# Block 0's second feed-forward product in plain float32, with w_out split piece by piece behind it

## The chip, the cores and the metric

The kernel runs on one core of a Trainium2 chip. The metric is the device time of one execution, in microseconds. Five engines work side by side, each through its own row of instructions in a fixed order: TensorE (PE, with the weight loads PEld), VectorE (DVE), ScalarE (ACT), GpSimd (POOL) and SyncE (SP), which here only starts DMAs. PE writes to PSUM, the others work in SBUF and, apart from GpSimd, in PSUM. An instruction that needs another engine's result waits at the head of its row, and everything behind it waits too.

## What is computed

A linear attention with positive random features, and behind it a feed-forward layer with GELU, all in float32:

```python
def phi(x):
    proj = np.einsum('bhsd,md->bhsm', x, omega)
    sq = np.sum(x * x, axis=-1, keepdims=True) / 2.0
    h = proj - sq
    h = h - np.max(h, axis=-1, keepdims=True)
    return np.exp(h) / np.sqrt(m)
...
num = np.einsum('bhsm,bhmd->bhsd', q_p, kv)
den = np.einsum('bhsm,bhm->bhs', q_p, z)[..., None] + 1e-06
x = (num / den).transpose(0, 2, 1, 3).reshape(B * S, H * D)
h = x @ w_in
g = 0.5 * h * (1.0 + erf(h * inv_sqrt2))
return (g @ w_out).astype(np.float32)
```

Batch 8, 8 heads, 576 tokens a batch, head dimension 64, 128 features; 4608 tokens in all, w_in 512 x 2048, w_out 2048 x 512.

## The kernel before

**Two streams.** The attention runs in 32 units: a batch and a pair of heads. The first four units (mode 0, batch 0) and the next four (mode 1, batch 1) compute with plain float32 matmuls; the others (mode 2) with operands split into two narrower halves. The feed-forward part runs in 12 blocks of 384 tokens. For a block, 16 chunks c of 128 hidden features go by: `mm1` gives h (12 matmuls: w_in high and low by x high and low), `act_high` the GELU, and `mm2`, two chunks later, adds the chunk's part to three accumulators of 128 tokens by 512 columns.

**Precision by halves.** Matmul operands of type fp32r are narrower than float32. So a product is made of three: high by high, low by high, high by low. For the second product, `act_high` writes g (line 629) and its fp32r cast gh (630, ScalarE), `act_low` the rest gl (635, VectorE), and `mm2` issues lines 645 to 647: woh by gh, woh by gl, wol by gh.

**The weights.** Both weight matrices come as 64-bit words in 16 pieces each, are turned into float32 on the chip and split into halves, in the steps of `w_events`: `w_load` (line 124, a DMA into one of three buffers raw), `w_scale` (131 and 132, ScalarE), `w_bits` (136 and 137, VectorE), `w_round` (141, GpSimd, which also frees the raw buffer), `w_high` (148 on GpSimd or 152 on ScalarE for w_out by turns, 148 or 150 for w_in) and `w_low` (155, on VectorE for w_out, on GpSimd for w_in). The float32 piece stands in one of two buffers wb, and the halves wih, wil, woh, wol stay for the whole kernel.

**A mode-1 unit.** `proj_mid` projects (533, 544) and takes the maximum (594) and the difference (596) on VectorE into the one tile et; `exps` (320, ScalarE); `kv_plain` (571, PE; its copy 574), `kvz_plain` (581, copies 586 and 587 on VectorE); `q_trans` (439, PE, which reads et) and `q_copy` (446); `num` (459), `den` (475), `div` (485 to 494) to the feed-forward's input xs. For a mode-2 unit GpSimd makes r (242), the parts of v (343 to 361), the shift of k (266) and kh (373).

**What sets the order.** Every step is put on a list with a time by hand (`at`), one unit of time being roughly one product step of PE; the list is sorted, and a scheduler lays it out on the engines' rows, moving steps that are ready into places that it believes idle. Block 0's chunk c is due at 6c and its second product at 6c + 15.3; piece i of w_out has its steps at 5.5i. The mode-1 units are due at 5, 25.5, 46 and 66.5, the first mode-2 unit at 115, with its preparation from 85. So block 0, the mode-1 units and nearly all of the weight pieces share the first sixth of the run.

Of the kernel before, what the change touches and what calls it, by code (L numbers as in the profile page):

```python
# [19 lines left out]
P = 128  # L20
T = 384
# [7 lines left out]
def favor_attention_ffn(ctx: ExitStack, tc: tile.TileContext, qT, kT, v, omT, w_in, w_out, out):  # L29
# [31 lines left out]
    wih = cp.tile([P, NJ, F], F32R, name="wih")  # L61
    wil = cp.tile([P, NJ, F], F32R, name="wil")
    woh = cp.tile([P, NF, DM], F32R, name="woh")
    wol = cp.tile([P, NF, DM], F32R, name="wol")
    xt = cp.tile([P, 2, 2, S], F32, name="xt")
    xf = xt.rearrange("p a h s -> p (a h s)")
    x2 = xt[:, :, 0]
# [32 lines left out]
    def need(*ks):  # L100
        assert all(k in done for k in ks), ks
# [30 lines left out]
        nc.scalar.activation(pc.lo, pc.lo.bitcast(U32), AF.Copy, scale=2.0 ** -29)  # L132

    def w_bits(pc):
        pc.b = dp[0].tile([P, pc.n], I32, tag="wb", name="wb", bufs=2)
        nc.vector.tensor_scalar(pc.b, pc.hi, 3, None, op0=ALU.logical_shift_left)
        nc.vector.scalar_tensor_tensor(pc.b, pc.hi, -2 ** 31, pc.b, op0=ALU.bitwise_and, op1=ALU.bitwise_or)  # L137

    def w_round(pc):

        nc.gpsimd.tensor_tensor(pc.b, pc.b, pc.lo, op=ALU.add)  # L141

    def w_high(pc):
        pc.w = pc.b.bitcast(F32)
        if pc.win:
            pc.w = pc.w.rearrange("p (j w) -> p j w", j=NJ)
        if pc.e[0] is nc.gpsimd:
            nc.gpsimd.tensor_scalar(pc.wh, pc.w, 1.0, 1.0, op0=ALU.mult, op1=ALU.mult)
        elif pc.e[0] is nc.vector:
            nc.vector.tensor_copy(pc.wh, pc.w)  # L150
        else:
            nc.scalar.copy(pc.wh, pc.w)
# [5 lines left out]
    def piece(win, i, n):  # L158
        pc = Obj()
        pc.win, pc.n, pc.i = win, n, i  # L160

        if win:
            pc.e = (nc.gpsimd, nc.gpsimd) if i < WEARLY else (nc.vector, nc.gpsimd)
        else:
            pc.e = (nc.scalar, nc.gpsimd)[i % 2], nc.vector
        if win:
            m = n // NJ
            sl = slice(i * m, (i + 1) * m)
            pc.src, pc.wh, pc.wl = wi_raw[:, :, 2 * i * m:2 * (i + 1) * m], wih[:, :, sl], wil[:, :, sl]
        else:  # L170
            c, r = divmod(i * n, DM)
            pc.src, pc.wh, pc.wl = wo_raw[:, c, 2 * r:2 * (r + n)], woh[:, c, r:r + n], wol[:, c, r:r + n]
        return pc

    def w_events(pc, t, ts):
        for fn, dt in zip((w_load, w_scale, w_bits, w_round, w_high, w_low), ts):
            at(t + dt, fn, pc)
# [445 lines left out]

    def act_high(n, c):
        h = hs.pop((n, c))
        g = mp[0].tile([P, T], F32, tag="g", name="g", bufs=1)
        gh = mp[0].tile([P, T], F32R, tag="gh", name="gh", bufs=3)
        gl = mp[0].tile([P, T], F32R, tag="gl", name="gl", bufs=3)
        nc.scalar.activation(g, h[:, 0:T], AF.Gelu)  # L629
        nc.scalar.copy(gh, g)  # L630
        gs[n, c] = (g, gh, gl)
# [4 lines left out]
        done.add(('g', n, c))  # L636

    def mm2(n, c, i, c0=0, c1=DM):
        need(('w', False, c), ('g', n, c))
        if c == 0:  # L640
            accs[n, i, c0] = ps_at() if c0 else ps_acc()
        acc = accs[n, i, c0][:, 0:c1 - c0]
        _, gh, gl = gs[n, c]
        s = slice(i * P, (i + 1) * P)
        nc.tensor.matmul(acc, gh[:, s], woh[:, c, c0:c1], start=(c == 0), stop=False)  # L645
        nc.tensor.matmul(acc, gl[:, s], woh[:, c, c0:c1], start=False, stop=False)  # L646
        nc.tensor.matmul(acc, gh[:, s], wol[:, c, c0:c1], start=False, stop=(c == NF - 1))  # L647
        done.add(('a', n, c, i, c0))

    def store(n, i, c0=0, c1=DM):  # L650
        need(*[('a', n, c, i, c0) for c in range(NF)])
        if c0 == 0:
            os[0] = mp[0].tile([P, DM], F32, tag="raw", name="o", bufs=3)
        o = os[0][:, c0:c1]
        nc.vector.tensor_copy(o, accs.pop((n, i, c0))[:, 0:c1 - c0])
        nc.sync.dma_start(out[n * T + i * P:n * T + (i + 1) * P, c0:c1], o)
# [29 lines left out]

    for i in range(NF):
        w_events(piece(True, i, 512), BASE + 1 + 5 * i if i < WEARLY else SUB * i - 27, (-6, 0, 1, 2, 3, 4))
        w_events(piece(False, i, 512), 5.5 * i, (-7, 0, 1, 2, 3, 4))


    bursts = [5 + 20.5 * k for k in range(NJ)] + [115 + 35 * k for k in range(len(units) - 2 * NJ)]
# [53 lines left out]
    for n in range(NBLK):  # L746
        for j in range(NJ):
            t = n * NF * SUB - (5, 4, 3, 3)[j]
            at(t, block_high, n, j)
            at(t + 0.6, block_low, n, j)  # L750
        for c in range(NF):
            t = (n * NF + c) * SUB
            for s in range(3):

                at(t + s + 0.3 if (n, c) != (0, 1) or s == 2 else 1.5 + 0.3 * s, mm1, n, c, s)
            at(t + 3.4, act_high, n, c)
            at(t + 4.5, act_low, n, c)
            if (n, c) >= (NBLK - 1, NF - 1 - LAG):
                continue
            for i in range(NTT):  # L760
                for cut in cuts(n, i):
                    at(t + SUB * LAG + 3.3 + i, mm2, n, c, i, *cut)
                    if c == NF - 1:
                        at(t + SUB * LAG + 4 + i, store, n, i, *cut)
# [50 lines left out]
```

## Time and profile before

| | us |
|---|---|
| median of three runs | 1100.27 (1098.75 to 1100.88) |
| the profiled execution's own time | 1100.79 |
| its span, first to last instruction | 1098.9 |
| busy: PE, VectorE, ScalarE, GpSimd | 1049.1, 789.7, 618.0, 482.4 |
| mean granted PE clock | 0.992 |

PE is busy for 95% of the span. Its records overlap, since matmuls are pipelined and their ends are modelled, so its share of busy time says little about short stops; the distance from one start to the next says more. A row of the windows view gives, for a stretch of time, each engine's busy time with its number of instructions, the granted PE clock as a fraction, and the DMA engines' share and rate. A row of the groups view gives line, engine, operation, out<-in, shapes and count, then busy time, mean length in ns, and idle time of the engine just before, with what ended it. A timeline row gives start, length, engine and line, with idle time before it in brackets. "SPq" is SyncE issuing a DMA.

### The profile page before, as it was taken

How to read it: one execution, taken by the hardware profiler on the slowest of the kernel's cores; microseconds unless marked ns; L12 is line 12 of the kernel's file. 1: busy time of each engine (PE TensorE's matmuls, PEld its weight loads, DVE VectorE, ACT ScalarE, POOL GpSimd, SP SyncE). 2: the span in 40 equal slices, each digit the busy share in tenths (PEclk: the TensorE clock that was granted, in tenths of full speed). 3: DMA queues.
4: the chain of work that ended last, by engine and by line, in shares of the span. 5: the costliest groups of instructions: out<-in, count | busy, mean ns of one | idle time of the engine just before them, and what ended most of it. 6: DMA issues, size and time to landing. Idle time of an engine off the chain costs nothing.

```text
span 1098.9 us, 17294 instructions
## 1 busy us (share of the span) xinstructions
PE 1049.1 (95%) x6022; PEld 906.3 (82%) x6022; DVE 789.7 (72%) x1780; ACT 618.0 (56%) x1310; POOL 482.4 (44%) x554
## 2 busy tenths in 40 slices
PE   8897899999999999999899999999999999999998
PEld 6675678888888888888778788878888888998998
DVE  5879887778878887877888878888887877411211
ACT  7856665666556466666546666654666655322321
POOL 4624546544455565444456544445654444000000
PEclk9989999999999999999999999999999999999999
DMA  8534532211211211211212211122121110000000
GB/s 232 169 110 150 164 117 60 70 44 44 75 44 56 84 56 52 62 50 47 72 56 56 75 32 56 57 62 55 56 74 41 49 63 1 1 29 1 30 1 30
DMA packets 46279, 70.92 MB, mean 65 GB/s; under 512 B 13680, under 2 KB 22256, under 8 KB 46192
## 3 DMA queue, kind: packets, MB, share of 16 engines
q1 hardware_dynamic: 46192, 69.81, 21.2%
q8 instruction: 48, 0.79, 0.3%
q14 instruction: 39, 0.32, 0.1%
HBM read 60.36 MB, written 9.44 MB: 64 GB/s over the span
## 4 chain that ended last, share of the span: by engine, by line
PE 64%; DVE 18%; ACT 2%; issue 2%; POOL 1%; POOLq 0%; ACTq 0%; DVEq 0%
PE h L622 27%; PE acc L647 9%; PE acc L646 9%; PE acc L645 9%; PE at L468 3%; PE at L400 3%; DVE gl L635 2%; DVE et L285 2%; PE at L249 2%; DVE mx L287 2%; PE at L277 1%; DVE xs L497 1%; DVE rt L485 1%; DVE rc L486 1%; DVE rt L488 1%
## 5 line engine op out<-in xcount | busy, mean ns | idle before, releaser
L622 PE MATMUL h<-xh,wih 128*128 128x384 f32 x768 | 263.2, 343 | 0.0
L622 PE MATMUL h<-xl,wih 128*128 128x384 f32 x768 | 262.5, 342 | 0.0
L622 PE MATMUL h<-xh,wil 128*128 128x384 f32 x768 | 262.0, 341 | 0.0
L645 PE MATMUL acc<-woh,gh 128*128 128x512 f32 (+1 forms) x576 | 230.8, 401 | 0.0
L647 PE MATMUL acc<-wol,gh 128*128 128x512 f32 (+1 forms) x576 | 226.6, 393 | 0.0
L646 PE MATMUL acc<-woh,gl 128*128 128x512 f32 (+1 forms) x576 | 226.2, 393 | 0.0
L635 DVE TENSOR_TENSOR gl<-g,gh 128x384 fp32r<-128x384 f32 x192 | 128.6, 670 | 121.1 <-ACT gh L630 120.6
L242 POOL TENSOR_TENSOR r<-xt,r 64x256 fp32r<-64x256 f32 (+2 forms) x216 | 173.8, 813 | 59.5 <-ACT r L236 46.4
L629 ACT ACTIVATE g<-h 128x384 f32<-128x384 f32 x192 | 94.4, 491 | 170.0 <-PE h L622 161.0
L373 POOL TENSOR_SCALAR kh<-et 128x256 f16<-128x256 f32 (+1 forms) x120 | 50.2, 425 | 280.8 <-ACT et L320 176.0
L622 PEld LDWEIGHTS h<-xh,wih 128*128 128x128 f32 x768 | 145.1, 189 | 7.7 <-issue 1.8
L622 PEld LDWEIGHTS h<-xh,wil 128*128 128x128 f32 x768 | 145.0, 189 | 6.3 <-issue 0.9
L622 PEld LDWEIGHTS h<-xl,wih 128*128 128x128 f32 x768 | 145.3, 189 | 1.3 <-issue 0.9
L647 PEld LDWEIGHTS acc<-wol,gh 128*128 128x128 f32 x576 | 108.3, 188 | 23.9
L645 PEld LDWEIGHTS acc<-woh,gh 128*128 128x128 f32 x576 | 108.5, 188 | 14.6 <-issue 1.5
L646 PEld LDWEIGHTS acc<-woh,gl 128*128 128x128 f32 x576 | 108.6, 189 | 12.8 <-issue 0.4
L236 ACT CAST r<-xt 128x256 fp32r<-128x256 f32 (+2 forms) x216 | 88.2, 410 | 51.9 <-PE at L277 44.2
L630 ACT CAST gh<-g 128x384 fp32r<-128x384 f32 x192 | 98.8, 515 | 3.3
L381 DVE SCALAR_TENSOR_TENSOR kl<-et,kh 128x256 f16<-128x256 f32 (+1 forms) x120 | 65.2, 559 | 30.7 <-POOL kh L373 28.9
L327 DVE STREAM_TRANSPOSE qt<-et 128x288 f32<-128x288 f32 x96 | 45.2, 471 | 51.8 <-ACT et L320 51.4
L141 POOL TENSOR_TENSOR wb<-wb,raw 128x512 int32<-128x512 int32 x32 | 44.0, 1376 | 67.5 <-DVE wb L137 30.3
L254 ACT COPY lo<-at 128x256 f32<-128x256 f32 (+1 forms) x120 | 41.9, 349 | 55.4 <-PE at L249 53.5
(151 smaller groups left out, 1850.2 us busy)
## 6 DMA issues: line engine op xcount, KB each, us to landing
xt<-in_kT SPq DMA_DIRECT2D x56, 288.0 KB, 3.9
xt<-in_qT SPq DMA_DIRECT2D x56, 288.0 KB, 3.8
v<-in_v SPq DMA_DIRECT2D x32, 320.0 KB, 3.1
out_x<-o SPq DMA_DIRECT2D x35, 256.0 KB, 2.1
raw<-in_w_in SPq DMA_DIRECT2D x16, 512.0 KB, 3.9
raw<-in_w_out SPq DMA_DIRECT2D x16, 512.0 KB, 3.6
out_x<-o SPq DMA_DIRECT2D x2, 128.0 KB, 1.7
om<-in_omT SPq DMA_DIRECT2D x2, 32.0 KB, 2.1
```

Of the source, the lines that this page charges most:

```text
L236: nc.scalar.copy(u.r[i][:, 0:b - a], xf[:, a:b])
L242: nc.gpsimd.tensor_tensor(r, xf[D:, a:b], r, op=ALU.subtract)
L327: nc.vector.transpose(u.qt[g], ef[:, slice(*XG[NK + g])])
L373: nc.gpsimd.tensor_scalar(kh[:, :n], es, KSC, 1.0, op0=ALU.mult, op1=ALU.mult)
L381: nc.vector.scalar_tensor_tensor(kl[:, :n], es, KSC, kh[:, :n], op0=ALU.mult, op1=ALU.subtract)
L622: nc.tensor.matmul(h[:, 0:T], w, (xh, xh, xl)[k], start=(i == 0), stop=(i == 3 * NJ - 1))
L629: nc.scalar.activation(g, h[:, 0:T], AF.Gelu)
L630: nc.scalar.copy(gh, g)
L635: nc.vector.tensor_tensor(gl, g, gh, op=ALU.subtract)
L645: nc.tensor.matmul(acc, gh[:, s], woh[:, c, c0:c1], start=(c == 0), stop=False)
L646: nc.tensor.matmul(acc, gl[:, s], woh[:, c, c0:c1], start=False, stop=False)
L647: nc.tensor.matmul(acc, gh[:, s], wol[:, c, c0:c1], start=False, stop=(c == NF - 1))
```

## The change

Block 0's second product takes g as plain float32 (g0, written once by the GELU) and the float32 weight piece itself; the three matmuls become one. The cast gh and the difference gl fall away for block 0. A w_out piece no longer passes through wb: its float32 form is a tile of its own, in a ring of 17 that the low halves wol use too, as the float32 pieces come free. The high half of w_out is now always made by ScalarE, the low half by GpSimd; both are listed at 60 + 6i and 61 + 6i in place of 5.5i + 3 and 5.5i + 4. The output tiles get a name and two buffers of their own in place of three.

```diff
-    wol = cp.tile([P, NF, DM], F32R, name="wol")
+    wol, wo32 = [None] * NF, [None] * NF
+    def wo_tile(dtype, name):
+        return cp.tile([P, DM], dtype, tag="wo", name=name, bufs=NF + 1)
...
     def w_bits(pc):
-        pc.b = dp[0].tile([P, pc.n], I32, tag="wb", name="wb", bufs=2)
+        if pc.win:
+            pc.b = dp[0].tile([P, pc.n], I32, tag="wb", name="wb", bufs=2)
+        else:
+            pc.b = wo_tile(I32, f"wo32_{pc.i}")
...
+        if not pc.win:
+            wo32[pc.i] = pc.b.bitcast(F32)
+            done.add(('w32', pc.i))
...
+        if not pc.win:
+            wol[pc.i] = pc.wl = wo_tile(F32R, f"wol{pc.i}")
...
-            pc.e = (nc.scalar, nc.gpsimd)[i % 2], nc.vector
+            pc.e = nc.scalar, nc.gpsimd
...
     def act_high(n, c):
         h = hs.pop((n, c))
+        if n == 0:
+            gs[n, c] = mp[0].tile([P, T], F32, tag="gh", name="g0", bufs=3)
+            nc.scalar.activation(gs[n, c], h[:, 0:T], AF.Gelu)
+            done.add(('g', n, c))
+            return
...
+        if n == 0:
+            nc.tensor.matmul(acc, gs[n, c][:, s], wo32[c][:, c0:c1], start=(c == 0), stop=(c == NF - 1))
+            return
...
-            os[0] = mp[0].tile([P, DM], F32, tag="raw", name="o", bufs=3)
+            os[0] = mp[0].tile([P, DM], F32, tag="o", name="o", bufs=2)
...
-        w_events(piece(False, i, 512), 5.5 * i, (-7, 0, 1, 2, 3, 4))
+        w_events(piece(False, i, 512), 5.5 * i, (-7, 0, 1, 2, 60 + 0.5 * i, 61 + 0.5 * i))
...
-            at(t + 4.5, act_low, n, c)
+            if n:
+                at(t + 4.5, act_low, n, c)
```

Line numbers move with the diff (594 becomes 607, 596 becomes 609, 571 becomes 584). On TensorE, the first chunk's second product with the first mode-1 unit's products behind it, before:

```order
L645 MATMUL acc<-woh,gh 128x512
L646 MATMUL acc<-woh,gl 128x512
L647 MATMUL acc<-wol,gh 128x512
L571 MATMUL at<-et,v 65x128 x10
L533 MATMUL at<-om_66,xt 128x128 x8
L581 MATMUL at<-ident,kvt 128x65 x2
```

The first three rows stand there three times, once for each 128 tokens. Now (g0 is printed as g):

```order
L635 MATMUL h<-xl,wih 128x384
L665 MATMUL acc<-wo_0_741,g_791 128x512 x3
L584 MATMUL at<-et,v 65x128 x10
L546 MATMUL at<-om_66,xt 128x128 x8
L594 MATMUL at<-ident,kvt 128x65 x2
```

Nine matmuls became three, and nothing else moved there. On VectorE, the rows ahead of the third mode-1 unit's maxima and differences (594 and 596), before:

```order
L137 SCALAR_TENSOR_TENSOR wb<-raw,wb 128x512
L206 MEMSET v 128x10
L155 TENSOR_TENSOR wol<-wb,woh 128x512
L207 MEMSET v 64x1
L208 MEMSET v 64x1
L150 CAST wih<-wb 128x4x128
L136 TENSOR_SCALAR wb<-raw 128x512
L137 SCALAR_TENSOR_TENSOR wb<-raw,wb 128x512
L635 TENSOR_TENSOR gl<-g,gh 128x384
L594 TENSOR_REDUCE nm<-at 128x4 x2
L596 TENSOR_TENSOR et<-at,nm 128x512 x2
L586 COPY kvz<-at 128x2x64
```

Now (wo_8 is the float32 tile of piece 8 of w_out):

```order
L145 SCALAR_TENSOR_TENSOR wb<-raw,wb 128x512
L220 MEMSET v 64x1
L221 MEMSET v 64x1
L144 TENSOR_SCALAR wo_8_1214<-raw 128x512
L145 SCALAR_TENSOR_TENSOR wo_8_1214<-raw,wo_8_1214 128x512
L163 CAST wih<-wb 128x4x128
L607 TENSOR_REDUCE nm<-at 128x4 x2
L609 TENSOR_TENSOR et<-at,nm 128x512 x2
L599 COPY kvz<-at 128x2x64
```

The subtractions wol and gl are gone, the pieces' bits (136 and 137, now 144 and 145) stay. Between this unit's copy of kvz and the one before, the row now holds seven pieces' bits in place of six, in the next such stretch ten in place of seven, and in the last one of the four a single piece in place of five. On GpSimd, where the weight pieces end and the first mode-2 unit begins, before:

```order
L141 TENSOR_TENSOR wb<-wb,raw 128x512 x2
L148 TENSOR_SCALAR woh<-wb 128x512
L343 TENSOR_SCALAR vb<-v 128x10x64
L242 TENSOR_TENSOR r<-xt,r 64x256
L349 TENSOR_TENSOR v<-v,vb 128x640
L242 TENSOR_TENSOR r<-xt,r 64x256
L355 TENSOR_SCALAR vb<-v 128x10x64
L242 TENSOR_TENSOR r<-xt,r 64x256
L361 TENSOR_TENSOR vb<-v,vb 128x10x64
```

Now:

```order
L149 TENSOR_TENSOR wo_15_1592<-wo_15_1592,raw 128x512
L168 TENSOR_TENSOR wol_1791<-wo_7_1146,woh 128x512
L168 TENSOR_TENSOR wol_1851<-wo_8_1214,woh 128x512
L168 TENSOR_TENSOR wol_1890<-wo_9_1266,woh 128x512
L255 TENSOR_TENSOR r<-xt,r 64x256 x3
L168 TENSOR_TENSOR wol_1925<-wo_10_1338,woh 128x512
L356 TENSOR_SCALAR vb<-v 128x10x64
L362 TENSOR_TENSOR v<-v,vb 128x640
L368 TENSOR_SCALAR vb<-v 128x10x64
L374 TENSOR_TENSOR vb<-v,vb 128x10x64
L168 TENSOR_TENSOR wol_2032<-wo_11_1414,woh 128x512
L168 TENSOR_TENSOR wol_2109<-wo_12_1464,woh 128x512
```

The low halves of pieces 10 to 15 now stand among the first mode-2 unit's steps; the last three follow further down, up to that unit's kh. ScalarE's row has the sixteen casts woh from just ahead of block 0's last xh on, three, four, six and three in the four stretches between those copies.

More of the change, by code (lines that the diff above doesn't have):

```diff
@@ L170, in piece @@
         else:
-            c, r = divmod(i * n, DM)
-            pc.src, pc.wh, pc.wl = wo_raw[:, c, 2 * r:2 * (r + n)], woh[:, c, r:r + n], wol[:, c, r:r + n]
+            assert n == DM
+            pc.src, pc.wh = wo_raw[:, i], woh[:, i]
         return pc
@@ L638, in mm2 @@
     def mm2(n, c, i, c0=0, c1=DM):
-        need(('w', False, c), ('g', n, c))
+        need(('w', False, c) if n else ('w32', c), ('g', n, c))
         if c == 0:
@@ L642, in mm2 @@
         acc = accs[n, i, c0][:, 0:c1 - c0]
+        s = slice(i * P, (i + 1) * P)
+        done.add(('a', n, c, i, c0))
+        if n == 0:
+            nc.tensor.matmul(acc, gs[n, c][:, s], wo32[c][:, c0:c1], start=(c == 0), stop=(c == NF - 1))
+            return
         _, gh, gl = gs[n, c]
-        s = slice(i * P, (i + 1) * P)
         nc.tensor.matmul(acc, gh[:, s], woh[:, c, c0:c1], start=(c == 0), stop=False)
         nc.tensor.matmul(acc, gl[:, s], woh[:, c, c0:c1], start=False, stop=False)
-        nc.tensor.matmul(acc, gh[:, s], wol[:, c, c0:c1], start=False, stop=(c == NF - 1))
-        done.add(('a', n, c, i, c0))
+        nc.tensor.matmul(acc, gh[:, s], wol[c][:, c0:c1], start=False, stop=(c == NF - 1))
     def store(n, i, c0=0, c1=DM):
```

## The prediction

> **What bounds the kernel now.** I read the busy time by windows first. The four stretches below each run from one mode-1 unit's copy of kvz (L586, VectorE) to the next one's, 115.5 us in all, and hold the first 30 of block 0's 48 second products. The last row is a hundred microseconds of the later kernel, for comparison.
>
> ```profile
> core 0: us, PE busy (x) PEld busy (x) DVE busy (x) ACT busy (x) POOL busy (x), PEclk, DMA share, GB/s
> 50.89:79.87 28.98, 26.09 (x156) 21.57 (x156) 19.77 (x48) 18.43 (x31) 10.39 (x10) 0.88 0.28 87
> 79.87:107.70 27.83, 20.71 (x138) 15.58 (x137) 24.85 (x48) 17.33 (x28) 13.51 (x11) 0.98 0.49 148
> 107.70:137.79 30.09, 25.59 (x163) 20.52 (x162) 27.29 (x53) 19.07 (x31) 16.06 (x12) 0.95 0.56 170
> 137.79:166.40 28.61, 27.29 (x160) 21.39 (x158) 22.68 (x40) 18.32 (x32) 13.17 (x12) 0.95 0.36 109
> 400.00:500.00 100.00, 97.99 (x560) 86.34 (x559) 81.92 (x191) 61.84 (x132) 56.11 (x66) 1.00 0.21 60
> ```
>
> Later PE is busy 98 of 100 us at full clock, so there the kernel goes as fast as PE, and a microsecond won earlier is kept. In the second and third stretches VectorE is busy 52 of 58 us, PE only 46, and PE's clock is cut. The change works here. The groups by line over these four stretches, then the timeline around the longest stop:
>
> ```profile
> L141 POOL TENSOR_TENSOR wb<-wb,raw 128x512 int32<-128x512 int32 x23 | 32.0, 1392 | 49.8 <-DVE wb L137 18.8 <-issue 11.8 <-ACT kvt L574 6.7
> L137 DVE SCALAR_TENSOR_TENSOR wb<-raw,wb 128x512 int32<-128x512 int32 x22 | 22.4, 1019 | 0.2
> L155 DVE TENSOR_TENSOR wol<-wb,woh 128x512 fp32r<-128x512 f32 x15 | 13.8, 918 | 8.6 <-POOL woh L148 8.1
> L136 DVE TENSOR_SCALAR wb<-raw 128x512 int32<-128x512 int32 x22 | 10.9, 501 | 1.4 <-ACT raw L131 1.4
> L155 POOL TENSOR_TENSOR wil<-wb,wih 128x512 fp32r<-128x512 f32 x8 | 10.6, 1320 | 4.2 <-DVE wih L150 4.2
> L635 DVE TENSOR_TENSOR gl<-g,gh 128x384 fp32r<-128x384 f32 x12 | 8.9, 745 | 1.3 <-ACT gh L630 1.2
> L439 PE MATMUL at<-ident,et 128*128 128x128 f32 x35 | 7.3, 336 | 9.1 <-DVE et L596 9.1
> L630 ACT CAST gh<-g 128x384 fp32r<-128x384 f32 x13 | 6.7, 512 | 0.1
> L148 POOL TENSOR_SCALAR woh<-wb 128x512 fp32r<-128x512 f32 x8 | 5.7, 706 | 0.7
> L152 ACT CAST woh<-wb 128x512 fp32r<-128x512 f32 x7 | 4.3, 619 | 10.5 <-POOL wb L141 10.3
> ```
>
> ```profile
> 99.19 0.38 SPq L124 DMA_DIRECT2D raw<-in_w_in  x1
> ...
> 102.98 1.39 POOL L155 TENSOR_TENSOR wil<-wb,wih 128x512 fp32r<-128x512 f32 x1 [0.54 <-DVE wih L150]
> ...
> 103.27 1.64 DVE L137 SCALAR_TENSOR_TENSOR wb<-raw,wb 128x512 int32<-128x512 int32 x1
> ...
> 104.84 0.54 DVE L635 TENSOR_TENSOR gl<-g,gh 128x384 fp32r<-128x384 f32 x1
> ...
> 105.31 1.28 DVE L594 TENSOR_REDUCE nm<-at 128x4 f32<-128x512 f32 x2
> ...
> 106.51 1.27 DVE L596 TENSOR_TENSOR et<-at,nm 128x512 f32<-128x512 f32 x2
> ...
> 107.33 1.08 PE L439 MATMUL at<-ident,et 128*128 128x128 f32 x4 [5.06 <-DVE et L596]
> ...
> 109.03 0.68 DVE L137 SCALAR_TENSOR_TENSOR wb<-raw,wb 128x512 int32<-128x512 int32 x1
> ...
> 109.85 1.36 POOL L141 TENSOR_TENSOR wb<-wb,raw 128x512 int32<-128x512 int32 x1 [2.63 <-ACT raw L132]
> ...
> 111.24 0.33 SPq L124 DMA_DIRECT2D raw<-in_w_out  x1
> ```
>
> PE stood 5.06 us because L596 was late in VectorE's row, behind weight pieces and gl. The wol and gl subtractions, with the waits before them, hold VectorE 13.8 + 8.6 + 8.9 + 1.3 = 32.6 us of 115.5. That is the most that can be won here.
>
> A second thing paces the stretches: the three raw buffers. SyncE's own waits show it:
>
> ```profile
> SPq L124 <- POOL wb L141: 61.8, 19, 8.3
> ```
>
> Every load of a weight piece waits for GpSimd's rounding of the piece three earlier. Above, the buffer loaded at 99.19 is free after the rounding at 109.85 and is loaded again at 111.24: a turn of 12.05 us for three pieces, 4.0 us a piece in the busiest part. Over the stretches it was 115.5 / 23 = 5.0.
>
> **The change, part by part.** *The product.* Plain float32 stands in the attention: L571 is ten matmuls in the program and 20 records here. Behind it stands the chain of waits in the last blocks, where PE never stops.
>
> ```profile
> 16.70 0.66 PE L459 MATMUL at<-qh,kvz 128*64 128x288 f32 x4
> 17.18 0.66 PE L459 MATMUL h<-qh,kvz 128*64 128x288 f32 x4
> ...
> 19.48 2.40 PE L571 MATMUL h<-et,v 128*65 128x128 f32 x20
> ```
>
> ```profile
> 1003.58 2.09 PE h L622 x12
> 1005.67 0.23 PE acc L645
> 1005.90 0.23 PE acc L646
> ```
>
> L571 goes on by (2.40 - 0.27) / 19 = 0.11 us a record of 128 columns (0.27 us is one record's own length). L459's four records are two products on two halves of the columns, side by side: 0.48 us for two records deep, 0.24 us for 288 columns. The line through both gives 0.24 + 224 x 0.0008 = 0.43 us for 512 columns, two records 0.86 us. Four times L571's 0.11 x 4 would be 0.90, the upper end; the lower end is 0.84. Three fp32r products take 3 x 0.233 = 0.70 us. So each of the 48 products costs PE 0.16 us more, 7.7 us in all. Counted in the order, 30 fall into the four stretches, where PE has room, and 18 behind them: **+2.9 us** (2.5 to 3.6).
>
> The Trainium skill, "Perfetto Trace Analysis", section "Engine Utilization", rates the array at half its output rate for FP32_LOW_HIGH. If that held for a whole product it would cost 2 x 0.233 = 0.47 us; here each of the two records already takes that, so the trace bears it out only for a record.
>
> *First stretch and just before it.* There VectorE waits for a w_out half to come from GpSimd or ScalarE, with the attention's work behind it:
>
> ```profile
> 47.82 1.09 DVE L155 TENSOR_TENSOR wol<-wb,woh 128x512 fp32r<-128x512 f32 x1 [1.20 <-ACT woh L152]
> ...
> 55.68 1.49 DVE L155 TENSOR_TENSOR wol<-wb,woh 128x512 fp32r<-128x512 f32 x1 [1.72 <-POOL woh L148]
> ...
> 58.56 1.87 PE L533 MATMUL at<-om,xt 64*128 64x128 f32 x8 [1.92 <-DVE xs L494]
> ```
>
> Both are gone. The first is worth 0 to 2.3 us; I take the wait, **-1.2**. The second gives xs 1.72 + 1.49 = 3.2 us earlier. PE's clock of 0.88 in this stretch costs 0.12 x 28.98 = 3.5 us, and half of that should go with its stops: **-5.0** (0, if PE waits for something else, to -8, VectorE's busy time of 19.8 and a margin).
>
> *Second and third stretches.* VectorE loses seven wol and seven gl: 7 x 0.918 + 7 x 0.745 = 11.6 us. But the changed row has 7 + 10 pieces' bits here in place of 6 + 7, since pieces move ahead: 4 x (1.019 + 0.501) = 6.1 us come in. VectorE's floor is 52.1 - 11.6 + 6.1 = 46.6. The raw ring now needs more: of 17 pieces three are loaded ahead, and the other 14 go at a turn's pace. The turn of 12.05 less the gl in it (0.54) gives 3.83 us a piece, 53.7 us against 57.9: **-4.2**. Both ends: at the mean pace of 5.0, 70.3 us (+12.4); at VectorE's floor, -11.3. I take the busiest turn, because it comes from the same work with only the subtractions taken out.
>
> GpSimd gets the low halves here: in the stretches ten more instructions of 1.32 us, less eight of 0.71, +7.6 us on 53. It is not full, but it stops VectorE: L137 took 1.64 us when GpSimd's L155 (102.98 to 104.37) was running, 0.68 at 109.03. Per piece that is already in the 1.019. The Trainium skill, "SBUF — State Buffer", section "SBUF: two separate sides", says that the two engines share a port pair held for a whole instruction, so that the loser fully blocks. The trace agrees: 1.64 ends 0.54 after GpSimd's instruction does. By that rule the ten added instructions could stop VectorE for up to 13.2 us: its floor in the two stretches would be 59.8 at most, 1.9 over today's time, and the sum 1096 in place of the 1090 that the rows give.
>
> *Fourth stretch.* Of the row's five pieces one is left. VectorE: 22.7 - 5 x 0.918 - 3 x 0.745 - 5 x 1.52 = 8.3 us, no bound. PE by the pitches: 48 of L622 at 0.174 = 8.4, nine products at 0.86 = 7.7, L571 2.2, L459 1.9, the rest 2.0: 22.2. With some 1.8 us of stops 24.0, against 28.6: **-4.6** (0 to -6.4).
>
> *Handover to mode 2.* Six low halves (6 x 1.32 = 7.9 us) now stand on GpSimd among the first mode-2 unit's work, whose row before has room, for example
>
> ```profile
> 176.63 0.74 POOL L242 TENSOR_TENSOR r<-xt,r 64x256 fp32r<-64x256 f32 x1 [3.71 <-ACT r L236]
> ```
>
> Behind a low half waits r, behind r the projections on PE. I take **+1.0** (0 to 7.9), nearer to nothing, since most of it fits into such gaps and PE has blocks 0 and 1 to work on.
>
> *At nothing.* ScalarE: 13 casts of 0.512 go, nine more of 0.619 come, on 73 us busy of 115; the first casts of w_out stay early, in block 0, so "behind it" holds for the low halves alone. SyncE's loads are the same 32. Two output buffers in place of three: a block's third copy waits for the first one's landing.
>
> ```profile
> out_x<-o SPq DMA_DIRECT2D x35, 256.0 KB, 2.1
> ...
> 1094.77 0.42 DVE L655 COPY o<-acc 128x256 f32<-128x256 f32 x1 [0.37 <-PE acc L647]
> ```
>
> PE's next block covers that: it needs the third bank only after twelve L622 (2.09 us) and two more accumulators. Without that cover each of eleven inner block ends could cost some 0.4 us (4 us).
>
> **The sum**, against this profile's own execution of 1100.8 us (the median of the runs is 1100.3): +2.9 - 1.2 - 5.0 - 4.2 - 4.6 + 1.0 = -11.1, **1090 us**.
>
> **Rivals.** *All the slack goes:* stretches two and three fall to VectorE's floor (-11.3), the first by 8, the fourth to PE's 22.2, the wait ahead by 2.3, the handover is free: -28.0 + 2.9 = -25.1, 1076. For it: PE waits for VectorE alone in the big stops. Against: loads waited for GpSimd 61.8 us.
>
> *The ring wins (slower):* raw has three buffers as before, and the changed row asks for 17 pieces where 13 were. At the mean pace of 5.0 us the two stretches take 70.3: +12.4 - 5.0 - 4.6 - 1.2 + 3.9 = +5.5, 1106. It decides against the change above 64.8 us, 4.6 us a piece. Against it: the slow turns were those in which VectorE was stuck behind wol.
>
> *GpSimd late at the handover:* all 7.9 us show, 1097.
>
> *A product at half price:* if one record's worth of passes were the whole cost, 0.47 us, the 18 products would gain 0.23 us each, -4.1 in place of +2.9: 1083. The L459 and L571 rows speak against it. (This is what the rule of the Trainium skill's "Perfetto Trace Analysis", above, would make of the product.)
>
> That the change does not do what it says is excluded by the order: one plain matmul stands for three, and no gl of block 0 is left.
>
> **Chances.** My forecast 0.52, all slack 0.18, handover late 0.14, ring slower 0.12, half price 0.04. Two in ten may be left out: the far half of the first rival and most of the ring's, so 1080 to 1101. A measurement here can tell about 0.2%, 2.2 us, from no change. Faster than that: 0.50 + 0.18 + 0.04 + most of the late handover, 0.83. Same: 0.07, from the edges of three cases. Slower: 0.10, the ring.
>
> **What would show it.** L439's wait for L596 falls from 9.1 us to under 4; the fourth stretch is near 24 us; the second and third together near 54, with SyncE still waiting for the rounding; the product's records run at 0.43 us; behind the fourth stretch the kernel is some 3 to 4 us longer than before. Wrong would be: records of another pitch; two stretches of over 60 us; r on GpSimd waiting behind low halves while PE stands.

## The result, and the profile after

The changed kernel takes 1111.45 us (median of four runs, 1111.06 to 1111.79) against 1100.58 us before: the ratio is 1.0102 (95% interval 1.0085 to 1.0120). It is some 11 us slower, where some 11 us faster had been forecast. The profiled execution took 1111.16 us, its span is 1109.4 us.

The busy time by windows of the changed kernel, with the same cuts as before (from one mode-1 unit's copy of kvz, now L599, to the next), then the stretch from the fourth cut to block 1's fifth chunk in both kernels:

```profile
51.15:78.66 27.51, 23.52 (x150) 18.42 (x151) 19.13 (x46) 19.20 (x31) 10.51 (x10) 0.99 0.42 130
78.66:104.59 25.93, 24.31 (x133) 14.84 (x132) 21.07 (x44) 16.30 (x27) 13.19 (x10) 0.94 0.52 158
104.59:141.41 36.82, 29.43 (x158) 19.62 (x156) 29.01 (x51) 22.04 (x37) 24.87 (x19) 0.91 0.48 154
141.41:163.39 21.98, 21.93 (x123) 14.11 (x122) 10.39 (x25) 11.64 (x20) 12.91 (x12) 1.00 0.27 68
163.39:203.80 40.41, 40.41 (x182) 28.66 (x182) 23.10 (x52) 19.31 (x42) 20.50 (x21) 1.00 0.20 59
```

```profile
166.40:200.30 33.90, 33.28 (x175) 28.32 (x176) 23.75 (x56) 18.49 (x40) 16.17 (x18) 1.00 0.22 69
```

The third stretch is the surprise: 36.8 us where it was 30.1. The fourth is short (22.0), but behind it PE has 40.4 us of work in place of 33.9.

The rest of the run is best read as a delay: the start of a chunk's first product (L635, before L622) less its start in the profile of before. "2, 4" is block 2, chunk 4. The other kernels in the table, on which the argument rests, are explained below.

| | block 0, chunk 8 | 1, 0 | 1, 4 | 2, 0 | 2, 4 | 4, 4 | 6, 4 | 7, 4 | 11, 0 |
|---|---|---|---|---|---|---|---|---|---|
| start in before, us | 123.8 | 182.0 | 200.3 | 263.6 | 287.2 | 459.5 | 638.4 | 724.1 | 1024.3 |
| changed kernel | +2.5 | +2.1 | +3.5 | +3.5 | +7.6 | +7.7 | +10.0 | +10.7 | +10.5 |
| before_o2 | -1.8 | -1.8 | -1.8 | -1.9 | +2.2 | +2.3 | +4.0 | +4.7 | +4.5 |
| om_lo | +1.3 | +3.4 | +5.2 | +5.3 | +5.3 | +5.5 | +5.5 | +5.6 | +6.7 |
| h_bits12 | +1.7 | -2.3 | -1.0 | -1.0 | +3.1 | +3.2 | +4.8 | +5.5 | +5.3 |
| hb12_om | +1.5 | -2.5 | -0.7 | -0.7 | -0.7 | -0.5 | -0.5 | -0.3 | +0.7 |
| hb10_om | -0.6 | -4.7 | -3.2 | -3.2 | -3.2 | 0.0 | +0.3 | +0.4 | +1.5 |
| bh10 | -1.7 | -6.1 | -6.1 | -6.1 | -6.1 | -6.1 | -5.6 | -5.6 | -5.7 |

The profile of before (1100.79 us) is slower than most executions of that kernel: before_o2 (explained below), whose VectorE row is the same up to block 0's output, is 1.8 us ahead of it there. So every row looks some 2 us better than against a usual execution; the rows can be compared with one another.

So the loss has two parts of their own: 3.5 us by block 1, and 7.0 us in a few jumps behind it, where PE is the bound, the largest (4.1 us) at block 1's output. The timeline around that jump:

```profile
277.40 0.68 DVE L677 COPY o<-acc 128x512 f32<-128x512 f32 x1
...
278.77 0.68 DVE L677 COPY o<-acc 128x512 f32<-128x512 f32 x1
...
280.11 0.33 SPq L237 DMA_DIRECT2D v<-in_v  x1
280.50 0.90 SPq L678 DMA_DIRECT2D out_x<-o  x2
281.51 0.61 SPq L236 DMA_DIRECT2D xt<-in_qT  x1
284.21 0.69 DVE L677 COPY o<-acc 128x512 f32<-128x512 f32 x1 [3.22 <-DMA out_x<-o]
284.81 0.47 DVE L501 STREAM_TRANSPOSE rt<-rc 128x288 f32<-128x288 f32 x1
285.21 0.44 DVE L298 STREAM_TRANSPOSE et<-at 128x288 f32<-128x288 f32 x1
285.70 0.40 PE L481 MATMUL at<-qh,kvh 128*128 128x288 f32 x1 [3.15 <-DVE et L298]
```

Read it downwards. The first two output copies are done at 278.1 and 279.5, but their DMAs stand in SyncE's queue behind the load of v, which itself waits until 280.1 for GpSimd's L374, and leave only at 280.5. The third copy has no third buffer and waits in VectorE's row until 284.21. L298 stands behind it, and PE waits for L298. The windows view shows what the stop costs besides:

```profile
282.00:286.00 4.00, 0.85 (x5) 0.41 (x4) 1.77 (x4) 0.90 (x2) 2.63 (x3) 1.00 0.73 266
286.00:290.00 4.00, 4.00 (x15) 3.36 (x14) 3.37 (x9) 1.19 (x3) 0.73 (x1) 0.57 0.39 118
```

In the 4 us behind the stop PE was granted 0.57 of its clock (from 286.54 to 289.95, 3.41 us, it is 0.50), and the jump of 4.1 us is longer than the stop of 3.15. The Trainium skill, "TensorE: Matmul & The Clock Gate", Part 1, says that the clock falls to half after an idle window of about 3.4 us and comes back after a busy one. The half clock and its return agree; the stop itself was shorter than that window.

The third stretch, by the chain of waits in it (start, length, what; a piece named "issue" is time that no shown wait explains), and PE's three longest stops in the four stretches, from its timeline:

```profile
110.24 1.12 DVE wb L145
111.36 0.02 issue
111.38 0.63 ACT woh L165
112.01 0.03 issue
112.04 1.32 POOL wb L149
113.36 0.02 issue
113.38 0.04 DVE wih L163
113.42 0.31 issue
113.73 0.43 DVE wo L144
114.16 0.02 issue
114.18 1.63 DVE wo L145
115.81 1.20 DVE nm L607 x2
117.01 0.61 DVE et L609
117.62 0.14 issue
117.76 1.23 PE at L472 x4
```

```profile
78.29 1.06 PE L452 MATMUL at<-ident,et 128*128 128x128 f32 x4 [3.25 <-DVE et L609]
...
117.76 1.23 PE L472 MATMUL at<-qh,kvz 128*64 128x288 f32 x4 [4.20 <-DVE et L609]
...
141.04 1.23 PE L452 MATMUL at<-ident,et 128*128 128x128 f32 x8 [3.15 <-DVE et L609]
```

PE stands where it stood before, for the differences L609 (before L596). The forecast's first test was that this wait falls below 4 us; over the four stretches it is 7.4 + 4.7 = 12.1 us, against 9.1 + 2.8 = 11.9 before:

```profile
PE at L452 <- DVE et L609: 7.4, 3, 3.2
PE at L472 <- DVE et L609: 4.7, 2, 4.2
```

The wol and gl that were ahead of them are gone, but weight pieces stand in their place: at 110 to 116 us a rounding on GpSimd, wih, and both steps of a w_out piece's bits come ahead of the maxima L607. Ahead of the stop that ends at 141 us it is pieces 12, 13 and 14, pulled ahead one after the other.

### The profile page after: what moved, and what is told of

The parts are those of the page before. It is cut to its first block, busy times and chain, and to the rows that moved or that the text cites. A ratio compares the mean times of both kernels' runs of the same rounds, so it can differ in the third digit from the quotient of the medians.

```text
span 1109.4 us, 17161 instructions
## 1 busy us (share of the span) xinstructions
PE 1060.0 (96%) x5974; PEld 898.0 (81%) x5974; DVE 774.5 (70%) x1748; ACT 614.7 (55%) x1302; POOL 495.2 (45%) x562
## 4 chain that ended last, share of the span: by engine, by line
PE 69%; DVE 20%; ACT 3%; issue 3%; DMA 2%; POOL 1%; SPq 0%; POOLq 0%; ACTq 0%; DVEq 0%
PE h L635 28%; PE acc L670 9%; PE acc L669 9%; PE acc L668 9%; PE at L481 3%; PE at L413 3%; PE acc L665 2%; DVE gl L654 2%; DVE et L298 2%; PE at L262 2%; DVE mx L300 2%; PE at L290 2%; DVE rc L499 1%; DVE rt L498 1%; DVE rt L501 1%
## 5 line engine op out<-in xcount | busy, mean ns | idle before, releaser
L635 PE MATMUL h<-xh,wih 128*128 128x384 f32 x768 | 265.0, 345 | 0.0
L635 PE MATMUL h<-xl,wih 128*128 128x384 f32 x768 | 262.1, 341 | 0.0
L635 PE MATMUL h<-xh,wil 128*128 128x384 f32 x768 | 262.0, 341 | 0.0
L668 PE MATMUL acc<-woh,gh 128*128 128x512 f32 x528 | 211.5, 401 | 0.0
L670 PE MATMUL acc<-wol,gh 128*128 128x512 f32 x528 | 208.3, 395 | 0.0
L669 PE MATMUL acc<-woh,gl 128*128 128x512 f32 x528 | 208.0, 394 | 0.0
L654 DVE TENSOR_TENSOR gl<-g,gh 128x384 fp32r<-128x384 f32 x176 | 118.8, 675 | 114.9 <-ACT gh L649 114.3
L648 ACT ACTIVATE g<-h 128x384 f32<-128x384 f32 x176 | 86.5, 491 | 168.0 <-PE h L635 158.0
L635 PEld LDWEIGHTS h<-xh,wih 128*128 128x128 f32 x768 | 144.8, 189 | 9.0 <-issue 3.4
L635 PEld LDWEIGHTS h<-xh,wil 128*128 128x128 f32 x768 | 144.9, 189 | 8.4 <-issue 3.3
L635 PEld LDWEIGHTS h<-xl,wih 128*128 128x128 f32 x768 | 144.9, 189 | 1.0 <-issue 0.4
L670 PEld LDWEIGHTS acc<-wol,gh 128*128 128x128 f32 x528 | 99.6, 189 | 22.0
L668 PEld LDWEIGHTS acc<-woh,gh 128*128 128x128 f32 x528 | 99.8, 189 | 11.9 <-DVE o L677 0.4
L669 PEld LDWEIGHTS acc<-woh,gl 128*128 128x128 f32 x528 | 100.0, 189 | 11.4
L649 ACT CAST gh<-g 128x384 fp32r<-128x384 f32 x176 | 90.6, 515 | 3.1
L333 ACT ACTIVATE et<-et 128x2304 f32<-128x2304 f32 x28 | 59.6, 2130 | 3.3 <-DVE et L325 1.3
```

The lines of the kernel that those rows point to most:

```text
L333: nc.scalar.activation(et, et, AF.Exp)
L635: nc.tensor.matmul(h[:, 0:T], w, (xh, xh, xl)[k], start=(i == 0), stop=(i == 3 * NJ - 1))
L654: nc.vector.tensor_tensor(gl, g, gh, op=ALU.subtract)
L670: nc.tensor.matmul(acc, gh[:, s], wol[c][:, c0:c1], start=False, stop=(c == NF - 1))
```

## Experiments

The kernels are named as in the table. Each ratio is against runs of the kernel before on the same chip, with its 95% interval. The changed kernel has the ratio 1.0102. The kernel before took 1098.2 to 1100.6 us in the median, by chip, so kernels are compared by their ratios, and two whose intervals overlap widely are not told apart by their times; the delays and stretches, each from one execution, then say where they differ.

**The output buffers, on the kernel before (before_o2).**

```diff
-            os[0] = mp[0].tile([P, DM], F32, tag="raw", name="o", bufs=3)
+            os[0] = mp[0].tile([P, DM], F32, tag="o", name="o", bufs=2)
```

> The kernel before, with two output buffers in place of three and nothing else. Theory A (two output buffers stop VectorE's row at the end of a block, and the attention behind it): the copy of the output waits for the output DMA several us in all (0 with three buffers, 7.5 in the changed kernel), the first block end at which this happens costs some 4 us, and the time goes up by 5 to 8 us, to 1106-1108. Rival (the four jumps of the changed kernel come from its other rows): within 2 us of the kernel before, 1099-1102.

Measured: 1105.02 us, ratio 1.0058 (1.0038 to 1.0078). The view of the output copy's line shows the same wait as in the changed kernel:

```profile
its engine sat idle before it (us, times) until:
  PE acc L647: 12.0, 7
  DMA out_x<-o: 7.5, 7
```

and the delays jump at the same places: by 4.1 between blocks 2, 0 and 2, 4, by 1.7 up to 6, 4 and by 0.7 up to 7, 4, 6.4 us in all. So theory A holds. The 1.8 us that it is ahead at first are no gain: VectorE's row is that of before until the first output, and its first stretch took 27.4 us at a granted clock of 0.94 where the profile of before shows 28.98 at 0.88. The front part thus varies by some 2 us between executions.

**The third buffer back in the changed kernel (om_lo).** There is no room for it beside the ring of 17; it was taken from lo and rc, and from om32, which moved to a pool that is closed early.

```diff
-            os[0] = mp[0].tile([P, DM], F32, tag="o", name="o", bufs=2)
+            os[0] = mp[0].tile([P, DM], F32, tag="o", name="o", bufs=3)
-        u.lo[i] = p2().tile([P, 2, M], F32, tag="lo", name="lo", bufs=2)
+        u.lo[i] = p2().tile([P, 2, M], F32, tag="lo", name="lo", bufs=1)
-        rc = sp.tile([P, HS // 32], F32, tag="rc", name="rc", bufs=2)
+        rc = sp.tile([P, HS // 32], F32, tag="rc", name="rc", bufs=1)
```

> The changed kernel with three output buffers again; the room comes from one buffer lo and one rc in place of two, and from om32 in the pool that is closed early. Theory A (two output buffers cost the four jumps behind block 1): the copy's wait for the output DMA falls from 7.5 us to 0 and the delay against the kernel before grows by less than 1 us behind block 1, where it grew by 7.0; time 1104-1106, unless the single lo costs something itself, which would be seen as many small delays at the projections. Rival (the other rows are the cause): 1110-1113.

Measured: 1108.07 us, 1.0085 (1.0069 to 1.0102). The copy's wait for the DMA is gone and so are the jumps: +5.2 at block 1, 4 and still +5.6 at 7, 4. The time is above the expected 1104 to 1106: the front part came out 1.7 us later in this profile, and 1.1 us were added behind block 7. By the ratios alone (1.0085, 1.0102) a gain is not clear; it is the jumps that show it.

**What paces the third stretch: four first tries.** The first three are the high halves by turns (after_turns), a fourth raw buffer (after_raw4) and the low halves on VectorE (after_lowv):

```diff
-            pc.e = nc.scalar, nc.gpsimd
+            pc.e = (nc.scalar, nc.gpsimd)[i % 2], nc.gpsimd
```

> The changed kernel, with the high halves of w_out made by ScalarE and GpSimd by turns, as before, the low halves still on GpSimd. Theory S (the casts of w_out stand in ScalarE's row right behind the rounding, and the next piece's scaling waits behind them): ScalarE's wait in the casts for the rounding falls from 24.3 us in the four stretches to some 10-12, the third stretch falls from 36.8 us to 31-33, the time from 1111.4 to 1106-1108. Theory G (GpSimd is what paces the ring): eight more instructions of 0.7 us on GpSimd, third stretch 37-40, time 1111-1115.

Measured: 1112.00 us, 1.0112 (1.0089 to 1.0135); third stretch 37.4 us. ScalarE's wait in the casts stayed at 24.5 us in five waits in place of nine. Half the casts gone changed nothing, so theory S in this form fell.

```diff
-        pc.raw = dp[0].tile([P, 2 * pc.n], I32, tag="raw", name="raw", bufs=3)
+        pc.raw = dp[0].tile([P, 2 * pc.n], I32, tag="raw", name="raw", bufs=4)
```

> The changed kernel with four raw buffers in place of three. Theory R (the turn of the three buffers limits the pieces): SyncE's wait for the rounding falls from 70.7 us by half, the second and third stretches together from 62.7 to 55-58, the time to 1105-1107. Theory S (the rows of ScalarE, VectorE and GpSimd wait for one another piece by piece, in program order, whatever the number of buffers): stretches within 2 us of 62.7, time 1109-1113.

Measured: 1116.64 us, 1.0161 (1.0133 to 1.0189), slower than either theory gave. With a free buffer the scheduler pulls pieces still further ahead: 9 and 8 stand in the second and third stretch, and these took 30.1 and 33.9 us, 64.0 together. Low halves now reach GpSimd's row long before their tile in the ring is free:

```profile
POOL wol L168 <- PE acc L665: 17.5, 3, 7.5
```

(5.7 us in the changed kernel). So a fourth buffer does not help with this order. That three buffers hold the crowd back is argued from this, not shown, since the rows changed with the buffer.

```diff
-            pc.e = nc.scalar, nc.gpsimd
+            pc.e = nc.scalar, nc.vector
```

> The changed kernel with the low halves of w_out on VectorE, as before, and the high halves still on ScalarE alone. Theory G (GpSimd, with the low halves between the roundings, delays the ring and locks VectorE out): roundings come earlier, second and third stretches from 62.7 to 56-59, time 1105-1108. Theory S or V (ScalarE's casts, or VectorE's own load): VectorE gets up to 10 instructions of 0.92 us more in the stretches, these stay at 62-70, time 1111-1118.

Measured: 1111.43 us, 1.0109 (1.0085 to 1.0133); second and third stretch 61.0 us. Where the low halves are made makes no difference to the time that can be measured.

The fourth try (h_halves) takes all halves out of the way, by later places in the list and an order on ScalarE and GpSimd:

```diff
+            with tc.issue_after(last['s']):
                 nc.scalar.copy(pc.wh, pc.w)
...
+        with nullcontext() if pc.win else tc.issue_after(last['r']):
             pc.e[1].tensor_tensor(pc.wl, pc.w, pc.wh, op=ALU.subtract)
...
-        w_events(piece(False, i, 512), 5.5 * i, (-7, 0, 1, 2, 60 + 0.5 * i, 61 + 0.5 * i))
+        w_events(piece(False, i, 512), 5.5 * i, (-7, 0, 1, 2, 86 - 1.5 * i, 87 - 1.5 * i))
```

(last['s'] and last['r'] are the last piece's scaling and rounding.)

> The changed kernel, with all 16 high halves of w_out queued on ScalarE behind the last piece's scaling, and all 16 low halves on GpSimd behind the last piece's rounding, so that none of them stands between two pieces. Theory L (the halves, which wait in their rows for a rounding, 24.3 us, and for block 0's products, 5.7 us, hold up the pieces behind them): the third stretch falls from 36.8 us to 30-33, the time from 1111.4 to 1106-1109; 21 us of low halves come late on GpSimd, so up to 3 us of this may be given back at the handover. Theory V (the bits of the pieces ahead of the maxima in VectorE's row decide): third stretch 35-38, time 1110-1114.

Measured: 1109.70 us, 1.0102 (1.0087 to 1.0117); third stretch 36.0 us. Of the 6.7 us that the stretch grew by, theory L explains 1 at most, and the ratio is that of the changed kernel. A second use of this run: all 16 low halves now come at the handover to mode 2, and from the end of the fourth stretch to block 1's fifth chunk it takes 40.4 us, as in the changed kernel. GpSimd is not late there.

**Pieces held back.** In h_bits12 the bits of pieces 12 to 15 are queued on VectorE behind the third mode-1 unit's kvz, the end of the third stretch:

```diff
+        with tc.issue_after(last['z']) if not pc.win and pc.i >= 12 else nullcontext():
             nc.vector.tensor_scalar(pc.b, pc.hi, 3, None, op0=ALU.logical_shift_left)
             nc.vector.scalar_tensor_tensor(pc.b, pc.hi, -2 ** 31, pc.b, op0=ALU.bitwise_and, op1=ALU.bitwise_or)
```

> The changed kernel, with the bits of w_out's pieces 12 to 15 queued on VectorE behind the end of the third stretch: 7, 7 and 4 pieces in the second, third and fourth stretch in place of 7, 10 and 1. Theory V (pieces pulled ahead crowd the third stretch, while the fourth has room): third stretch from 36.8 us to 30-33, fourth from 22.0 to 23-26, the four together 1 to 4 us shorter, time 1107-1110. Theory N (a piece costs the same wherever it stands, some 1.6 us): third 32, fourth 27, sum and time as in the changed kernel, 1110-1113.

Measured: 1105.96 us, 1.0076 (1.0056 to 1.0096). Its third and fourth stretch:

```profile
104.50:136.10 31.60, 27.39 (x155) 18.80 (x154) 23.72 (x46) 20.20 (x35) 19.28 (x15) 0.95 0.54 162
136.10:158.90 22.80, 22.80 (x126) 14.70 (x125) 15.49 (x31) 13.21 (x24) 18.84 (x15) 1.00 0.34 87
```

The third becomes 5.2 us shorter, the fourth only 0.8 longer, and the stop of 3.15 us at 141 us is gone. A part of the 5.2 us is the granted clock, 0.95 in place of 0.91. Theory V holds: in the fourth stretch PE is the bound (busy for all of the 22.80 us), and pieces beside it are nearly free. The stop of 4.2 us in the third stretch stays. With both edits (h_both12),

> Both edits at once: halves behind the last scaling and rounding, and the bits of pieces 12 to 15 behind the third stretch. If L and V are both right and apart, the stretches fall by both, third to 28-31 and the four together from 112.2 to 105-108 us, time 1104-1107. If one theory alone is right, it is no better than that one's kernel.

the time is 1106.88 us, 1.0078 (1.0063 to 1.0093), the four stretches 110.4 us: no better than holding the bits alone. Holding at three places (pace; pieces 4 to 7, 8 to 10, 11 to 15),

> The changed kernel, with w_out's bits held on VectorE at three places: pieces 4 to 7 behind the end of the first stretch, 8 to 10 behind the second, 11 to 15 behind the third: 3, 6, 7 and 5 pieces in the four, where the changed kernel has 4, 7, 10 and 1. Theory V (VectorE's row ahead of the maxima is what sets a stretch, some 1.7 us for each piece): first 26, second 24.5, third 31, fourth 23-24; together 104-106 us (changed kernel 112.2), time 1103-1106. Theory N (only the crowd of three pieces at the end of the third stretch cost something): as with pieces 12 to 15 held alone, together 107-109, time 1105-1107.

gave 1105.57 us, 1.0062 (1.0046 to 1.0078), and stretches of 25.8, 25.6, 32.5 and 22.8, 106.7 in all: shorter by 1.3 us than with one hold, with the third not better. That lies between the two theories' sums and does not decide between them.

**Both remedies together (hb12_om, hb10_om, pace_om).**

> The changed kernel with the two remedies together: pieces 12 to 15 behind the third stretch, and three output buffers (one lo, one rc, om32 in the early pool). If the two losses are apart, they add: 1111.4 - 5.4 - 6.4 + 1.4 (what the single lo was seen to cost) = 1101, within 0.3% of the kernel before. If they are one loss seen twice: 1104-1106.

Measured: 1102.03 us, 1.0037 (1.0023 to 1.0051), near the expected 1101. In the table each remedy shows its own part: hb12_om is at -0.7 at block 1, 4, as h_bits12 is (-1.0), and loses 1.4 us from there to block 11, as om_lo does (1.5). So the losses are two. The ratios are too coarse for the sum itself: they fell by 0.26% and 0.17% for one remedy each and by 0.65% for both, each with an interval of some 0.15 to 0.2% to either side.

> As the one with both remedies, but pieces 10 to 15 are held behind the third stretch: 7, 5 and 6 pieces in the last three. Theory V: third stretch 28-29 us, fourth 24-25, together 1 to 2 us less than with 12 to 15 held, time 1099-1101. If a piece in the fourth stretch costs what it saves in the third: no difference, 1101.

Measured: 1101.24 us, 1.0029 (1.0018 to 1.0040); third stretch 29.2, fourth 22.7. The stretches are shorter, as by theory V; the time is not told apart from that of hb12_om.

> The three holds (4 to 7, 8 to 10, 11 to 15) together with three output buffers. By theory V 1097-1100; by theory N 1100-1102.

Measured: 1102.26 us, 1.0031 (1.0019 to 1.0043). Theory V's time was missed. So with both remedies the changed kernel is still 0.3% behind.

**What the rest is.** Three runs (hb10_k, hb10_ql, hb10_qt) take the room for the third output buffer from other tiles in place of lo, with pieces 10 to 15 held as in hb10_om:

```diff
-        kh = p2().tile([P, 2, M], F16, tag="kh", name="kh", bufs=2)
-        kl = p2().tile([P, 2, M], F16, tag="kl", name="kl", bufs=2)
+        kh = p2().tile([P, 2, M], F16, tag="kh", name="kh", bufs=1)
+        kl = p2().tile([P, 2, M], F16, tag="kl", name="kl", bufs=1)
```

> The changed kernel with pieces 10 to 15 held and three output buffers; the room comes from kh, kl and rc with one buffer each (lo keeps two) and from om32 in the early pool. Theory D (the single lo cost the 4.7 us that built up between block 2 and the end): the delay against the kernel before stays near -3 from block 1 on, time 1095-1098. Theory C (the change's core is behind by 0.3% whatever is mended): 1100-1102. A single kh and kl may cost something of their own, which would be seen as stops at the products of kh and kl.

> The same with the room taken from ql, three buffers in place of four (lo, kh, kl, rc as in the changed kernel). Theory D: 1095-1098. Theory C: 1100-1102.

> The same with the room taken from qt, one buffer in place of two. Theory D: 1095-1098, unless the single qt stops VectorE's transposes behind GpSimd's ql, which would be seen as waits of qt for ql. Theory C: 1100-1102.

Measured: 1123.59 us, 1.0240 (1.0220 to 1.0261); 1108.16 us, 1.0081 (1.0065 to 1.0097); 1115.09 us, 1.0146 (1.0125 to 1.0166). Each is worse than lo. Up to block 1, 4 the three stand at -4.1, -1.5 and -2.6, so the loss comes later, in mode 2. With one kh GpSimd waits before it for PE 122.5 us in 69 waits, before the change 96.4 in 41:

```profile
POOL kh L392 <- PE at L419: 122.5, 69, 5.1
```

Neither theory's time came out. What was shown is that kh with kl, ql and qt have no buffer to spare. Theory D had put hb10_om's 4.7 us between blocks 2 and 11 (-3.2 to +1.5) on the single lo, but hb12_om and om_lo, with the same single lo and rc, lose only 1.4 us there. The other 3.2 us come by block 4, 4, where hb10_om has waits that those two have not, 2.8 us in two between 285 and 470 us; their cause was not followed.

```profile
PE at L296 <- DVE rc L506: 2.8, 2, 1.9
```

The last question is whether holding pieces is a remedy for the change, or helps any kernel of this kind. The same hold of pieces 10 to 15 went into the kernel before (bh10):

> The kernel before (three matmuls, halves at once, three output buffers), with the bits of w_out's pieces 10 to 15 queued on VectorE behind the end of the third stretch. If the hold helps because it undoes what the change did to the row (theory V), the kernel before, whose row was never crowded so, gains at most 1 us: 1097-1099. If holding helps any kernel of this kind (its third stretch also falls by 2 to 3 us, its fourth has room): 1095-1097, and the changed kernel's core would then be that much worse than it.

Measured: 1093.48 us, ratio 0.9953 (0.9939 to 0.9967). It beats both kernels. Its third and fourth stretch:

```profile
105.38:132.12 26.74, 26.74 (x165) 21.74 (x164) 21.69 (x46) 17.84 (x29) 11.54 (x9) 0.90 0.49 152
132.12:159.96 27.84, 25.04 (x157) 19.80 (x156) 23.78 (x43) 17.41 (x29) 14.42 (x11) 1.00 0.54 149
```

PE has no stop left in the third, at whose end it stood 3.8 us before. My expectation for theory V, at most 1 us, was wrong: the kernel before lost to pieces ahead of the maxima too. This gives the fairest comparison on record of the two ways to make the product. With the same hold and three output buffers, the kernel before reaches block 2 at -6.1, the changed one (hb10_om) at -3.2. Of the -6.1, 1.7 us are there from the start, as in before_o2; the hold itself wins some 4.4 us by there.

## Why the prediction was wrong, step by step

The forecast's terms against the two profiles (span against span +10.5 us):

| step | forecast | measured | from |
|---|---|---|---|
| just before the first stretch | -1.2 | +0.3 | cuts 50.89 and 51.15 |
| first stretch | -5.0 | -1.5 | 28.98, 27.51 |
| second and third | -4.2 | +4.8 | 57.92, 62.75 |
| fourth, 18 products, handover | -0.7 | -0.1 | third cut to block 1, 4: 62.5, 62.4 |
| output buffers, "at nothing" | 0 | +7.0 | delay +3.5 to +10.5 |

**Right: the product.** A float32 product is two records, and its pitch is 0.43 us a record, from these rows of two and of four records:

```profile
128.51 1.02 PE L665 MATMUL acc<-wo,g 128*128 128x512 f32 x2
...
131.55 1.88 PE L665 MATMUL acc<-wo,g 128*128 128x512 f32 x4
```

(1.88 - 1.02) / 2 = 0.43 us. The forecast wrote 0.43 by a slip: its own 0.24 + 224 x 0.0008 is 0.42, which would have given +2.5, its lower end. Behind the fourth cut, up to block 1's fifth chunk, the groups by line show 36 records, 18 products, as counted: 18 x (0.86 - 0.70) = +2.9.

```profile
L665 PE MATMUL acc<-wo,g 128*128 128x512 f32 x36 | 17.2, 594 | 0.0
```

The rule of the Trainium skill's "Perfetto Trace Analysis", "Engine Utilization", holds for a record, not for the product, as the forecast had it.

**Right in sum, partly by luck: fourth stretch, products, handover.** The fourth stretch fell by 6.6 us in place of 4.6, but what follows up to block 1, 4 grew by 6.5 us in place of 2.9 + 1.0, because PE left work for later. The forecast gives the four stretches of before 30 second products; by the groups view they hold 33, and those of the changed kernel 30. So 18 stand behind the fourth cut in place of 15, 18 x 0.86 - 15 x 0.70 = 5.0 us, and with them 84 of L635 in place of 76 of L622, 8 x 0.174 = 1.4 us: 6.4 of the 6.5. For VectorE the forecast took off five pieces there, though one is left: 9.8 us, not 8.3, no bound either way. The handover's +1.0 was nearer to nothing (h_halves). That a full PE makes the price of a product visible was the right reading.

**Failed: "At nothing", two output buffers.** The forecast named the cover, "PE's next block needs the third bank only after twelve L622", and priced its loss at 4 us. The cover was the wrong one. PE does not need the bank; it needs what stands behind the copy in VectorE's row. The wait is not 0.4 us at each of eleven block ends but 3.2 us at one, where SyncE's queue also held the DMAs back (0.3 to 1.1 us at six others), plus the slow clock behind the stop. before_o2 shows 6.4 of the 7.0 us. At that kernel's two smaller jumps (1.7 and 0.7 us) the copy waits 0.31 us at most for a DMA; there VectorE's row itself stands in another order than before, and this was not followed further.

**Failed: "Second and third stretches", -4.2.** The step took a turn of the raw buffers, 3.83 us a piece, as the pace. The two stretches took 62.75 us, and over 60 was one of the forecast's own signs of being wrong. Its rival of a slow ring had the sign, but not the size (70.3 us), and the mechanism is not borne out: a fourth buffer made it worse. What decides is which pieces stand ahead of a unit's maxima in VectorE's row. The forecast had counted 17 pieces where 13 were and charged them to VectorE's busy time (6.1 us), which is not their position in the row. h_bits12, with the same pieces in other places, wins 5.2 of the 6.7 us by which the third stretch had grown.

A part of the relief was also spent: the bits of a piece became longer, with GpSimd now running the low halves beside them.

```profile
L145 DVE SCALAR_TENSOR_TENSOR wo<-raw,wo 128x512 int32<-128x512 int32 x14 | 16.4, 1169 | 0.2
...
L144 DVE TENSOR_SCALAR wo<-raw 128x512 int32<-128x512 int32 x14 | 8.4, 597 | 4.7 <-ACT raw L136 3.8 <-POOL wol L168 0.9
L145 DVE SCALAR_TENSOR_TENSOR wb<-raw,wb 128x512 int32<-128x512 int32 x8 | 6.4, 806 | 0.1
L144 DVE TENSOR_SCALAR wb<-raw 128x512 int32<-128x512 int32 x8 | 5.9, 737 | 7.9 <-ACT raw L136 7.9
```

37.1 us for 22 pieces, 1.69 us each, against (22.4 + 10.9) / 22 = 1.51 before: 3.8 us over the four stretches. The rule of the Trainium skill's "SBUF — State Buffer", section "SBUF: two separate sides", had been taken at 13.2 us at most; it points the right way, and the measured size is under a third. With the low halves on VectorE (after_lowv) a piece is back at 1.55 us, so they are most of it. That this costs time was not shown: neither after_lowv nor h_halves (1.60 us a piece) is faster than the changed kernel by more than the noise.

**Mis-sized: the first stretch and the wait ahead of it.** The stretch's 28.98 us in the profile of before is no fixed price of its rows; before_o2, with the same rows, took 27.4. About half of the clock's loss, of which the forecast wanted half back, was no property of the kernel. Against 27.4 the changed kernel's 27.51 is no gain. PE's stop of 1.92 us for xs is gone, but a new one of 3.25 us at the stretch's end (78.29) took what the vanished waits gave; with pieces 4 to 7 held (pace) the stretch is 25.8. Ahead of the stretch the wait of 1.20 us is gone, but PE stands 1.69 us for rc (until 51.57), and in this profile the granted clock from 37 to 45 us was 0.57 in place of 0.79, which is 1.8 us of those 8.

**The sign.** The slower case had been given 0.10, with one mechanism. Both losses belong to things that the change moves rather than adds, a buffer and the places of pieces. Mended together, the change still does not win: at block 2 it is 2.9 us behind the kernel before with the same hold (-3.2 and -6.1), about the price of its 18 products (2.9), with 2 us of spread between executions; that the products are the reason is argued from the size, not shown. What VectorE was relieved of did not come back as time; whether another order could win it was not tried.

## What to carry to other kernels

A buffer less is not covered because the engine that fills it has time: look at what stands behind the waiting instruction in its row, and at the queue that its DMA shares. Work that is taken off a busy in-order engine can be replaced by whatever the scheduler finds ready, as it was here, so price the new row at the place where someone waits, not the busy sum. Before a stall is charged to an edit, try holding ready work back on the kernel as it is: here that alone was worth 0.5%.

## What was not expected of the hardware

A stop of 3.15 us of PE is followed by 4 us at a granted clock of 0.57. A shorter stop can have the same price, and one as long can have none: the windows of the changed kernel around 638, 731 and 141 us, what follows a stop each, show 0.50 behind 2.57 us, full clock behind 1.47 us, and full clock behind 3.15 us too.

```profile
635.50:638.10 2.60, 0.08 (x1) 0.00 (x0) 2.46 (x3) 0.49 (x1) 2.52 (x2) 1.00 0.87 287
638.10:641.00 2.90, 2.85 (x8) 2.40 (x9) 2.68 (x8) 0.82 (x2) 1.09 (x2) 0.50 0.67 221
...
729.90:731.40 1.50, 0.04 (x1) 0.00 (x0) 1.50 (x4) 0.57 (x2) 1.42 (x3) 1.00 0.24 31
731.40:735.00 3.60, 3.60 (x20) 3.19 (x21) 2.95 (x7) 1.63 (x4) 3.52 (x3) 1.00 0.21 81
...
141.04:144.50 3.46, 3.41 (x19) 1.88 (x21) 2.53 (x5) 3.01 (x7) 3.30 (x4) 1.00 0.00 0
```

In h_halves the clock is 0.50 even behind a stop of 2.15 us (139.10). So the length of a stop alone does not decide; what does was not followed. The Trainium skill's page named above puts the idle window at some 3.4 us; 2.57 and 2.15 us lie below it, and the measurement decides.

One execution of the same rows can differ by 1.6 us in one stretch of 28 us, with the granted clock at 0.88 and 0.94.
